# A fused attention and token-mixing kernel: one load moved to ScalarE's queue, no filler between transposes, gate logits on VectorE, a narrower last eviction, and a new order of work

## The chip, the cores and the metric

The kernel runs on one core of a Trainium2 chip. A core has five engines that each work through a queue of their own: TensorE (PE in the profile; its weight loads are PEld), VectorE (DVE), ScalarE (ACT), GpSimd (POOL) and SyncE (SP), which here only issues DMAs. They wait for each other through semaphores. Data live in SBUF; matmuls write PSUM[...]. The time is device microseconds of one execution; the profile comes from one execution of its own, which was timed too.

## What is computed

x has 2048 tokens (S) of 512 channels (D), in bf16. Two branches are blended by a gate for each token.

```python
# A: causal attention in a sliding window of 256 tokens, 32 heads of 16 channels
q, k, v = split(x @ wqkv)                       # wqkv 512 x 1536
scores = einsum(q, k) * 16 ** -0.5              # kept where 0 <= query - key < 256
a = (softmax(scores) @ v).reshape(S, D) @ wo    # wo 512 x 512

# B: an MLP that mixes tokens
h = layernorm(x)                                # over channels, no weights
u = gelu(einsum("bsd,sf->bdf", h, w1) + b1)     # w1 2048 x 1376
y = (einsum("bdf,fs->bds", u, w2) + b2).transpose(0, 2, 1)   # w2 1376 x 2048

g = sigmoid((x * gate_w).sum(-1, keepdims=True))
out = g * a + (1 - g) * y
```

## The kernel before

**A list of tasks and an order written out.** The program is a list of tasks, each made by `add(name, {engine: cost}, emit, deps, ...)`: a group of instructions of one engine, the tasks it needs, the buffers or PSUM banks it takes, and a guess of its cost. `arrange(tasks)` at L85 puts them in order. It doesn't choose the engine or the order on an engine: both stand in `PLAN`, a table with one list of names per engine, in which a digit behind a colon is the PSUM bank or buffer to take. The set `THEN` names the steps after which a matmul step of 512 columns is issued in four row tiles of 128 x 32 (`tiled`) instead of one of 128 x 128. Costs and constants (`SWITCH`, `LATENCY`, `FETCH` and others) only steer in which sequence instructions of different engines are emitted and what the search for `PLAN` saw.

**The start.** x is loaded in groups of 128-token tiles by `load_x` (L449, DMA at L454): the first 512 tokens as x0.0 (tokens 0 to 255) and x0.2 (256 to 511), 256 KB each, the others as 512 KB. The query and key columns of wqkv come as four loads of 256 KB (wqk0 to wqk3, L470), the value columns as one (wv, L475). Everything goes out on SP's queue. The transposed x that the projections need is made by TensorE for the first 512 tokens (`emit_xt`, L605: 128 x 128 transposes, L608) and by transposing DMAs for the rest (xt1 to xt3, L463). TensorE begins with five matmuls of 512 zero columns (`warming`, L589, matmul at L591), which read the block `zeros` of 512 columns (L363, cleared at L518). Four transpose tasks of four 128 x 128 blocks follow, two for each half of the 512 tokens; between the halves stands `warmb`, three more matmuls of 256 zero columns. Each transpose task is copied out of PSUM by `copy_out` (L598, on ScalarE L602 or on VectorE L603).

**The middle.** `chain` (L655) makes every accumulation over several matmuls: projections q, k, v, the MLP's u (11 blocks of 128 features) and y (16 tiles of 128 tokens), each cut into steps of two matmuls that `PLAN` interleaves; all are recorded at L670. Attention runs in 16 query tiles and a few more groups: scores (s, L942, L998, L1042), exponentials on ScalarE (e, L894), masks on GpSimd or VectorE (m, L536, L974), weighted values (pv, L1087), then normalization by VectorE (n1 to n4 and nz, L1178 to L1213, which transpose back). Query evictions are multiplied by a parity column (QZ, L754). Layernorm statistics are L770 to L780. Evictions of the other projections and u may be on either engine (L438, L440, L602, L603).

**The gate.** For the first `NGP` = 1 block of 512 tokens the logits are 16 one-column matmuls (`emit_gate`, L799 to L805, recorded at L802; eviction L812). For the other tokens each 128-token tile is one fused multiply and sum on VectorE, task gl, L822. Then come an exponential (gatee) and the weights of the blend, c1 and c2.

**The end.** A y chain has 11 matmuls over features and four over wo and the normalized attention. f (L441 on VectorE, L438 on ScalarE) evicts it with c1 and c2, and o (L1305) stores it. The last tile is done in two halves of 256 columns, `y15l` and `y15r`.

## Time and profile before

| | |
|---|---|
| median of three runs | 200.57 us (199.84 to 200.81) |
| the profiled execution, timed | 199.82 us |
| its span, first to last instruction | 198.1 us |
| first matmul starts | 1.38 us |
| x0.0 landed, first transpose | 3.74, 3.79 us |
| first projection starts | 6.57 us |
| last matmul ends, about | 195.0 us |
| granted TensorE clock, mean | 1.00 |

Each line of the waits' view names an engine, its operation and what ended its wait, then total us, times and longest. A timeline line has start, duration, engine, line of the code, operation, and the operands with their shapes; a square bracket gives idle time ahead of it and what ended it. A group's row has total busy us and mean ns of one instruction. Durations of neighbours may overlap[...]; the time between two starts is the cost of one.

### The profile page before, as it was taken

What the parts mean: (1) busy time and instruction counts of PE and PEld (TensorE: products, weight loads), DVE (VectorE), ACT (ScalarE), POOL (GpSimd) and SP (SyncE); (2) the same over time, 40 slices, a digit from 0 to 9 for tenths busy, and PEclk for the clock granted to TensorE, in tenths of its full rate; (3) what the DMA queues carried; (4) which work ended last, traced back from release to release, by engine and by line L of the source; (5) the groups of instructions that cost most, each with busy time, mean ns of one, the idle gap of its engine ahead of it and who ended that gap; (6) DMA issues with size and microseconds to landing.
All of it is one profiled execution on the core that took longest, in us unless ns stands there. A gap on an engine that the chain in (4) does not pass through costs nothing. (4 is left out here: it accounts for less than half of the span.)

```text
span 198.1 us, 9100 instructions
## 1 busy us (share of the span) xinstructions
PE 193.0 (97%) x4058; PEld 93.3 (47%) x4058; DVE 156.5 (79%) x318; ACT 169.0 (85%) x198; POOL 80.0 (40%) x118
## 2 busy tenths in 40 slices
PE   7999999999999999999999999999999999999993
PEld 3643444353635445446543554344445354554572
DVE  1799888879998988986589799636867868869683
ACT  2369999999988996998999899899899989898632
POOL 6394897525344440214223200045069335452310
PEclk9999999999999999999999999999999999999999
DMA  5999798970060000001399770000211220200002
GB/s 156 294 284 232 131 319 278 346 187 0 8 174 18 18 0 3 3 5 32 98 364 367 280 210 3 26 26 30 68 37 58 60 68 22 62 30 30 30 3 83
DMA packets 23189, 22.02 MB, mean 111 GB/s; under 512 B 7566, under 2 KB 21262, under 8 KB 23150
## 3 DMA queue, kind: packets, MB, share of 16 engines
q1 hardware_dynamic: 23150, 21.44, 36.9%
q8 instruction: 32, 0.52, 1.1%
q14 instruction: 7, 0.06, 0.1%
HBM read 15.61 MB, written 2.10 MB: 89 GB/s over the span
## 5 line engine op out<-in xcount | busy, mean ns | idle before, releaser
L894 ACT ACTIVATE et<-ps 128x1024 bf16<-128x1024 f32 (+1 forms) x94 | 89.3, 1015 | 6.1 <-PE ps L942 2.4
L536 POOL TENSOR_SCALAR_AFFINE_SELECT et<-et 128x512 bf16<-128x512 bf16 (+2 forms) x63 | 46.7, 751 | 56.0 <-ACT et L894 40.9
L894 ACT ACTIVATE XT<-ps 128x1024 bf16<-128x1024 f32 (+1 forms) x60 | 58.1, 1011 | 7.3 <-PE ps L942 4.3
L670 PEld LDWEIGHTS <-wb 128*32 128x32 bf16 (+4 forms) x645 | 32.0, 97 | 34.5 <-issue 6.5
L670 PE MATMUL pb<-ug,wb 128*32 128x512 bf16 (+4 forms) x385 | 45.5, 366 | 0.0
L670 PE MATMUL pb<-h,wb 128*128 128x512 bf16 (+2 forms) x260 | 44.5, 381 | 0.0
L536 POOL TENSOR_SCALAR_AFFINE_SELECT XT<-XT 128x512 bf16<-128x512 bf16 (+1 forms) x28 | 20.0, 720 | 46.3 <-ACT XT L894 27.4
L670 PE MATMUL pb<-XT,wqkv 128*128 128x512 bf16 (+2 forms) x190 | 32.4, 372 | 0.4 <-DMA wqkv<-in_A_wqkv_dram 0.3
L1178 DVE STREAM_TRANSPOSE et<-ps 128x1024 f32<-128x1024 f32 (+1 forms) x17 | 20.1, 1183 | 11.9 <-PE ps L1087 11.1
L1087 PEld LDWEIGHTS <-VA 128*32 128x32 bf16 (+1 forms) x1056 | 20.1, 97 | 6.6 <-issue 1.5
L942 PE MATMUL ps<-QZ,KT 32*128 32x256 bf16 (+1 forms) x496 | 23.1, 265 | 0.0
L754 DVE TENSOR_TENSOR QZ<-pb,par 128x1024 bf16<-128x1024 f32 x16 | 19.5, 1221 | 3.2 <-PE pb L670 3.2
L670 PEld LDWEIGHTS <-wqkv 128*128 128x128 bf16 (+1 forms) x190 | 12.7, 98 | 14.6 <-DMA wqkv<-in_A_wqkv_dram 0.5
L670 PE MATMUL pb<-wo,xo 128*32 128x512 bf16 (+2 forms) x152 | 18.1, 375 | 0.0
L1087 PE MATMUL ps<-et,VA 128*32 128x128 bf16 (+2 forms) x624 | 17.9, 218 | 0.0
L942 PEld LDWEIGHTS <-KT 32*128 32x128 bf16 x496 | 7.4, 92 | 20.6 <-ACT et L894 10.7
L670 PE MATMUL pb<-wqkv,XT 128*128 128x512 bf16 (+1 forms) x70 | 16.5, 381 | 0.0
L974 DVE TENSOR_TENSOR et<-et,mask 128x512 bf16<-128x512 bf16 x26 | 13.3, 510 | 2.5 <-ACT et L894 2.4
L441 DVE TENSOR_SCALAR ot<-pb,c,c 128x512 bf16<-128x512 f32 (+1 forms) x11 | 8.6, 785 | 7.4 <-PE pb L670 7.3
L1087 PE MATMUL ps<-XT,VA 128*32 128x128 bf16 (+2 forms) x432 | 13.9, 215 | 0.0
L1087 PEld LDWEIGHTS <-VZ 128*32 128x32 bf16 x832 | 13.2, 98 | 0.7
L770 DVE BATCH_NORM_STATS2 stats<-xo 128x6 f32<-128x512 bf16 x16 | 10.7, 682 | 3.1 <-DMA xo<-in_A_x_dram 3.1
(76 smaller groups left out, 199.4 us busy)
## 6 DMA issues: line engine op xcount, KB each, us to landing
wb<-in_B_w_dram SPq DMA_DIRECT2D x8, 512.0 KB, 8.2
wb<-in_B_w_dram SPq DMA_DIRECT2D x2, 2048.0 KB, 9.2
VZ<-VA SPq DMA_DIRECT2D x26, 70.0 KB, 3.0
xo<-in_A_x_dram SPq DMA_DIRECT2D x3, 512.0 KB, 5.5
out_dram<-ot SPq DMA_DIRECT2D x12, 128.0 KB, 2.4
wb<-in_B_w_dram SPq DMA_DIRECT2D x4, 352.0 KB, 5.8
wqkv<-in_A_wqkv_dram SPq DMA_DIRECT2D x4, 256.0 KB, 5.0
wb<-in_B_w_dram SPq DMA_DIRECT2D x1, 1024.0 KB, 5.3
```

Source lines behind the costliest of these rows:

```text
L441: return nc.vector.tensor_scalar(out=out_, in0=in_, scalar1=scale, scalar2=bias, op0=ALU.mult, op1=ALU.add)
L536: return nc.gpsimd.affine_select(out=out_, in_=in_, pattern=[[0, n] for n in pattern] + [[step, HB]], compare_op=op, fill=0.0, base=base_, ...
L670: made.append(nc.tensor.matmul(buf(b)[c:z_, c0:c0 + w_], lhsT=lhsT[:, c:z_], rhs=rhs, start=(j == 0), stop=(j == n - 1), skip_group_check= ...
L754: lambda k=k, b=b: nc.vector.tensor_tensor(out=QZ[:, k, :, (i % NQ) * SB:(i % NQ + 1) * SB], in0=buf(b)[:, None, :].to_broadcast([P, 2, SB ...
L770: f"bs{t_}", {"DVE": 0.67}, lambda b=b, t_=t_: nc.vector.bn_stats(buf(b)[:], xo[:, t_, :]),
L894: lambda e=e, b=b, shape=shape: nc.scalar.activation(out=shape(buf(e)), in_=shape(buf(b)), func=ACT.Exp, scale=SCALE),
L942: made.append(nc.tensor.matmul(to[:, :, done:done + m], lhsT=keys(j if x == "A" else j - 1, k)[rows], rhs=q[rows], start=True, stop=True, ...
L974: made.append(nc.vector.tensor_tensor(out=v, in0=v, in1=m.to_broadcast(list(v.shape)), op=ALU.mult))
L1087: return lambda: nc.tensor.matmul(to(), lhsT=v() if callable(v) else v, rhs=buf(e)[rows, col:col + n], start=first, stop=last, tile_positi ...
L1178: lambda: nc.vector.transpose(out=view(buf(tr).bitcast(FP32)), in_=view(buf(o))), [last], takes=[tr], uses=[o],
```

## The change

The DMA of x0.2 is issued by ScalarE instead of SP, as the first instruction in ScalarE's list. The filler `warmb` between the transposes is gone. `zeros` has 128 columns, and the five warm-up matmuls read them repeated. `NGP` is 0, so the logits of the first four tiles are made by four more gl tasks on VectorE and no matmuls. The last tile is done in three parts of 256, 128 and 128 columns (l, m, r). `arrange` gets other costs: a price `TURN` for each pair of matmul forms instead of one `SWITCH`, `cost_of`, and another model of instruction fetch. `PLAN` and `THEN` are new throughout.

What the new lists do: on SP, gate_w and wv now come right after x1.4 and ahead of the transposing loads (before: x1.4, xt1, wv, x2.8, ...). Three of the four copies of transposed x are on VectorE (before: one). Thirteen evictions move from VectorE to ScalarE and as many back; 28 masks move from GpSimd to VectorE and 29 the other way. Value projections come earlier among the first projections. There are 3997 matmuls instead of 4058, and 167 changes of matmul form from step to step instead of 169.

```diff
-SWITCH = 0.095
+TURN = {
+    "d": dict(d=0, s=0.100, p=0.100, c=0.098, h=0.100),
...
+def cost_of(t, e):
...
 PLAN = dict(
     PE="""
-        warm:3 xta0.0.0:7 xta0.0.1:6 warmb xta0.1.1:4 xta0.1.0:5 q1_0.0:2 k3_0.0:3 k1_0.0:6 q3_0.0:1 k0_0.0:7
...
-        y14.11 y14.13 y13.13 y15r.6 y15r.8 y15l.11 y15l.13 y15r.10 y15r.11 y15r.13
+        warm:3 xta0.0.0:5 xta0.0.1:4 xta0.1.0:7 xta0.1.1:3 q1_0.0:0 q0_0.0:1 k3_0.0:6 q3_0.0:2 k1_0.0:5
+        k1_0.1 q0_0.1 k0_0.0:7 k1_0.2 k2_0.0:3 k2_0.1 k0_0.1 q1_0.1 k0_0.2 q3_0.1 q3_0.2 q3_0.3 k3_0.1
...
+        y15r.4 y15r.6 y14.13 y15l.4 y15l.6 y15l.8 y15l.10 y15l.11 y15l.13 y15m.0:4 y15r.8 y15r.10 y15r.11
+        y15r.13 y15m.2 y15m.4 y15m.6 y15m.8 y15m.10 y15m.11 y15m.13
     """,
     ACT="""
-        xtc0.0.1 xtc0.1.0 xtc0.1.1 kc3_0 kc1_0 kc0_0 kc2_0 e0.v0.0:4 e0.v0.1:5 kc3_1 e0.C.1:8 e0.C.0:a e-1.C.1:7
...
+        x0.2 xtc0.0.0 kc3_0 kc0_0 kc1_0 kc2_0 vc1 e0.v0.1:9 e0.v0.0:8 vc0 kc2_1 e0.C.1:1 e0.C.0:2 vc5
...
     DVE="""
-        const zeros bs3:1 xtc0.0.0 bs2:0 ba3 parity bs1:1 ba2 ba1 bs0:0 ba0 qc1_0 bs4:1 qc0_0 ba4 qc3_0 qc2_0 qc3_1
...
+        zeros bs1:1 bs3:0 ba3 bs0:0 xtc0.1.0 ba0 xtc0.1.1 bs2:0 ba1 xtc0.0.1 ba2 const parity qc3_0 bs6:0
...
     SP="""
-        x0.0 x0.2 wqk0 wqk1 wqk2 wqk3 x1.4 xt1 wv x2.8 bias xt3 x3.12 xt2 vs0 w1_02 w1_03 vs1 w1_22 vs2 gw w1_12
...
+        x0.0 wqk0 wqk1 wqk2 wqk3 x1.4 gw wv xt1 xt3 x3.12 x2.8 bias vs0 xt2 vs1 w1_11 w1_12 w1_00 w1_10
...
-    NGP = 1
+    NGP = 0
...
-    zeros = ug[:, 0, :]
+    zeros = ug[:, 0, 0:P]
...
                 src = X[t0 * P:(t0 + n_) * P].rearrange("(t p) d -> p t d", t=n_)
+                if t0 == 2:
+                    nc.scalar.dma_start(xo[:, t0:t0 + n_, :], src)
+                    return
                 nc.sync.dma_start(xo[:, t0:t0 + n_, :], src)
...
-            nc.tensor.matmul(buf(wu)[:, 0:w], lhsT=zeros[:, 0:P], rhs=zeros[:, 0:w], start=True, stop=True)
+            nc.tensor.matmul(
+                buf(wu)[:, 0:w].rearrange("p (a b) -> p a b", b=P), lhsT=zeros,
+                rhs=zeros[:, None, :].to_broadcast([P, w // P, P]), start=True, stop=True,
+            )
...
-    between = None
     for n_ in range(2):
-        if n_:
-            between = add("warmb", {"PE": 0.64}, lambda: warming(3, 256), [t], uses=[wu], ins=6)
...
-        parts = [("", 0, D)] if t_ < NT - 1 else [("l", 0, D // 2), ("r", D // 2, D)]
+        parts = [("", 0, D)] if t_ < NT - 1 else [("l", 0, D // 2), ("m", D // 2, 3 * D // 4), ("r", 3 * D // 4, D)]
```

## The prediction

> **What bounds the kernel now.** I read the page's busy shares first, then the waits of TensorE, then the timeline of its first and last microseconds, then windows, and last the rows of the operations that the change touches.

> ```profile
> span 198.1 us, 9100 instructions
> PE 193.0 (97%) x4058; PEld 93.3 (47%) x4058; DVE 156.5 (79%) x318; ACT 169.0 (85%) x198; POOL 80.0 (40%) x118
> ...
> PE pb L591 <- DVE ug L518: 1.4, 1, 1.4
> ...
> PE pb L670 <- DMA wqkv<-in_A_wqkv_dram: 0.3, 1, 0.3
> ...
> PE pb L670 <- ACT XT L894: 0.2, 1, 0.2
> ```

> The span is that of one profiled execution, timed at 199.82 us: 1.72 us lie outside it. TensorE is busy 97%, and its matmuls' listed waits (us in all, times, longest) are the 1.4 us before the first one, 0.3 us for the first weights and 0.2 us for an exponential. So a saving must come from TensorE's own work, from its start, or from what follows its last matmul. ScalarE may come next:

> ```profile
> 20.00:30.00 10.00, 10.00 (x110) 4.24 (x109) 8.68 (x28) 9.79 (x15) 8.96 (x15) 1.00 0.87 221
> ```

> This is a row of the windows view: PE, weight loads, DVE, ACT and POOL busy in 10 us, then clock, DMA share and GB/s. TensorE is full, ScalarE has 0.21 us left, and the DMA engines are at 0.87.

> The start, from the timeline (start, duration, engine, line):

> ```profile
> 3.79 1.03 PE L608 MATMUL pb<-ident,xo 128*128 128x128 bf16 x8
> 4.62 0.85 PE L591 MATMUL pb<-ug 128*128 128x256 bf16 x3
> 5.26 1.06 PE L608 MATMUL pb<-ident,xo 128*128 128x128 bf16 x8
> 6.57 7.25 PE L670 MATMUL pb<-XT,wqkv 128*128 128x256 bf16 x40 [0.26 <-DMA wqkv<-in_A_wqkv_dram]
> ...
> 4.44 0.69 DVE L770 BATCH_NORM_STATS2 stats<-xo 128x6 f32<-128x512 bf16 x1 [3.12 <-DMA xo<-in_A_x_dram]
> ...
> 0.81 0.97 SPq L454 DMA_DIRECT2D xo<-in_A_x_dram  x2
> 1.82 1.88 SPq L470 DMA_DIRECT2D wqkv<-in_A_wqkv_dram  x4
> 4.23 5.73 SPq L463 DMA_TRANSPOSE XT<-in_A_x_dram  x1
> 10.01 0.57 SPq L475 DMA_DIRECT2D wqkv<-in_A_wqkv_dram  x1
> ```

> The reader is to see that the first projection waits for weights, not for transposes, so the filler (three matmuls at 4.62) stands in time that TensorE has to wait anyway. A transposing DMA also holds SP's queue for 5.73 us, and the load of wv stands behind it.

> The gate's logits on TensorE, and what VectorE pays for the same (row: busy, mean ns):

> ```profile
> 23.02 0.54 PE L802 MATMUL pb<-gwc,XT 128*128 128x1 bf16 x16
> 23.43 1.02 PE L670 MATMUL pb<-wqkv,XT 128*128 128x512 bf16 x4
> ...
> L822 DVE SCALAR_TENSOR_TENSOR junk<-xo,gwr 128x512 bf16<-128x512 bf16 x12 | 8.3, 695 | 0.1
> L822 DVE DVE_READ_ACCUMULATOR junk<-xo,gwr 128x1 f32 x12 | 1.0, 81 | 0.0
> ```

> The end: the last matmuls stop at 195.04, and one eviction and one DMA follow.

> ```profile
> 191.21 0.72 DVE L1178 STREAM_TRANSPOSE et<-ps 128x512 f32<-128x512 f32 x1 [0.53 <-PE ps L1087]
> ...
> 193.85 0.60 PE L670 MATMUL pb<-wo,xo 128*128 128x256 bf16 x4
> 195.04 0.55 DVE L441 TENSOR_SCALAR ot<-pb,c,c 128x256 bf16<-128x256 f32 x1 [0.61 <-PE pb L670]
> ```

> [...] a 512-column matmul takes 427 ns in the warm-up and 216 ns later, and the 256-column projections drop from about 213 to 109 ns at 6.92 us. [...] Issues on SP stand 0.51 us apart, and the engines are 0.99 busy from 5 to 10 us; no run here shows a load from ScalarE. [...]

> **The change, part by part.** All sums stand against the profiled execution, 199.82 us; the median of the three shown runs, 200.57, is 0.75 above it.

> *Gate on VectorE.* TensorE loses 23.43 − 23.02 = 0.40 us, on the path: **−0.40**. VectorE gains 4 × (0.695 + 0.081) = 3.1 us. It stood idle in 21% of the span, but the four come before about 20 us, among the q evictions (1.22 us each) that free PSUM banks for the projections. With cover gone I would pay one such wait of at most 0.78. I take 0 for it, range 0 to +0.8.

> *Filler.* −0.64 us of TensorE's work (3 × 0.213), worth 0 while the projection waits for weights. [...]

> *x of tokens 256 to 511 from ScalarE.* SP no longer issues it, so the first weights are issued one slot (0.51 us) earlier, at 1.32. But the bytes are unchanged: x0.0, x0.2 and the first weights are 256 KB each on the same engines, and the weights (issued 1.82) landed at 6.53, the rest about 0.65 apart. Bounds 0 and −0.5; I take **−0.10**. x0.0 landed at 3.74 and x0.2 at 4.41; sharing from the start, x0.0 may come up to 0.67 later, inside the same cover of 0.26 + 0.64. On ScalarE the issue (about 0.5 us) comes ahead of everything, when it has nothing to do.

> *Copies of the transposes.* In before, one of the four runs on VectorE and three on ScalarE; now three run on VectorE, behind batch statistics. By its rows (0.69 each, the next starting 0.61 to 0.65 later): statistics of tiles 1, 3 and 0 from 3.8, copies of 0.41 from about 5.9 and 6.3, another statistics, and the last copy at about 7.4 to 7.9. Projections over that half of the channels are in PE's order from about 7.3. A new wait of 0 to 0.5; I take **+0.30**.

> *Form changes and order.* TensorE's steps are switches between tile forms: two matmuls of 512 columns take 0.432 before a step of the same form and 0.527 before another. The order goes from 169 to 167 switches and exchanges some tiled steps; with the median of each kind of step in the trace, the steps other than gate and filler sum to **−0.18**. Two gaps of before (0.33 in all at 113 us, 0.13 at 143) came from banks held by exponentials at just those places. The new order puts other steps there and may open gaps of its own; from −0.46 to +0.8, I take **−0.20**.

> *Moves between ScalarE and VectorE.* 13 evictions go each way, of near equal length (copies of 0.4 to 0.8); masks go 28 to VectorE and 29 to GpSimd. Net nothing where TensorE leads.

> *SP's order.* wv goes ahead of the first transposing DMA and its 5.73 us. Values are computed from 12.6 us instead of 16.6, by summing step durations from 6.5, and wv should land near 12. Behind it the xt1 load slips by the two loads put ahead of it: 0.64 MB at 291 GB/s is 2.2 us, from 12.06 to about 14.3; it is first used at 15.6. xt3 follows with an issue of 3.2 to 4.3 us, so about 17 to 18; first used at 17.6. Bounds 0 and +0.8, I take 0. wo, w1 and the exchanges of V are reordered by several us, against uses from 45 us on; nothing.

> *Tail.* The last eviction has 128 columns: 0.81 for 512 and 0.55 for 256 extrapolate to 0.41: −0.14; the last matmul is 0.05 shorter: **−0.19**. The one chain of 256 is now two of 128; a weight load with a one-column matmul took 25 ns in the gate, so loads don't bind (0.04, inside the −0.18). But fewer filler steps stand between the last pv step (190.64) and the tail that needs its normalized tile: 2.4 us by step durations, where the trace had 2.93, and VectorE's chain from 191.21 ended at 193.37, 2.46 with the pv step's end: **+0.15**.

> Zeros on 128 columns halve a memset of 0.27; TensorE starts about 0.15 earlier, and that is covered by x0.0. Sum: −0.40 − 0.10 + 0.30 − 0.18 − 0.20 − 0.19 + 0.15 = **−0.62 us**: 199.2 beside the profiled execution, and with the 0.75 a median of about 199.9.

> **The rivals.** About 0.5%, 1.0 us, is what a measurement of this kernel can tell from no change.

> *A, faster by more.* The copies cost nothing (−0.30), the weights land 0.5 earlier (−0.4 more), the old gaps go without new ones (−0.26): −1.58, so 199.0. For it: TensorE follows its own steps within 2.4 us over the whole trace. Against it: the DMA engines' 0.99 at the start.

> *C, ScalarE takes over.* With 9.79 of 10 us busy, exponentials set when banks come free, and TensorE's 0.58 turns into waits on ET and XT in 20 to 50 us: 200.5. Against it: the matmuls list 0.2 us of waits for exponentials in the whole span.

> *B, slower: [...]* The release at 6.92 followed a window of 3.41 us [...]:

> ```profile
> 3.51:6.92 3.41, 3.06 (x22) 2.36 (x22) 2.48 (x8) 1.16 (x3) 0.41 (x2) 1.00 0.91 299
> 0.10:3.51 3.41, 2.13 (x5) 0.58 (x5) 0.45 (x4) 1.28 (x1) 2.67 (x14) 1.00 0.42 126
> ```

> TensorE was 90% busy in it[...]. Without 0.64 us of filler the same window has 2.42 of 3.41, 71%; earlier projections may refill a few points. [...] matmuls stay at half speed until 10.3 us: 3.4 us at half rate lose 1.7. The copies' +0.30 is then hidden. −0.62 − 0.30 + 1.7 = +0.8: 201.4. [...]

> **How the numbers follow.** Forecast 0.40, own range 199.4 to 200.4; A 0.28; C 0.10; B 0.22, which stands also for a late xt3. Faster by over 0.5% (under 199.57): A and a quarter of the forecast's share, 0.38. Same: the rest of the forecast and C, 0.40. Slower: B, 0.22. The range 198.6 to 201.5 leaves out the outer parts of A and B.

> **What would show it.** The L802 row gone and L822 at 16; the first projection at 6.4 to 6.5; 256-column projections at 0.11 us from about 6.9 (B: from 10.3); a wait of PE for the XT copy of VectorE near 7.4 to 9; the wait of the last "wo" matmuls of the first part for VectorE, 0.1 to 0.2; a 128-column last eviction of 0.41. The forecast is wrong if TensorE's busy time outside the start doesn't fall by about 0.6, or if waits for xt3 or for banks of exponentials over 0.5 us stand in the middle.

## The result, and the profile after

The change makes the kernel slower: 202.47 us median (201.90 to 202.75) against 200.51 (199.84 to 200.81), ratio 1.0112, 95% interval 1.0086 to 1.0138. The time lies above the predicted range. Medians are of all timed executions of a kernel, while ratios leave out those over 1.5% above the kernel's fastest, so the two need not agree. The profiled execution took 202.45 us, its span is 200.7. First the page of the changed kernel, its busy shares and its DMA queues:

```profile
span 200.7 us, 8968 instructions
...
PE 192.7 (96%) x3997; PEld 92.4 (46%) x3997; DVE 155.6 (78%) x326; ACT 168.8 (84%) x198; POOL 73.6 (37%) x117
...
q8 instruction: 31, 0.51, 1.0%
q10 hardware_dynamic: 272, 0.26, 0.4%
```

```profile
PEld L979 <- issue: 3.4, 6, 1.4
...
PEld L1124 <- issue: 3.3, 5, 1.9
...
PE ps L1124 <- issue: 1.7, 1, 1.7
PE ps L979 <- issue: 1.2, 1, 1.2
...
PE pb L707 <- DMA wqkv<-in_A_wqkv_dram: 0.6, 1, 0.6
```

"issue" is time in which the engine waited for nothing that the profile shows. In the kernel before, the longest such wait on these two lines (there L942 and L1087) was 0.4 us. The timeline shows the places (start, duration, then engine, line and operands):

```profile
5.68 6.69 PE L707 MATMUL pb<-XT,wqkv 128*128 128x256 bf16 x36
12.95 1.02 PE L707 MATMUL pb<-wqkv,XT 128*128 128x512 bf16 x4 [0.58 <-DMA wqkv<-in_A_wqkv_dram]
...
40.82 0.11 PEld L979 LDWEIGHTS <-KT 32*128 32x128 bf16 x5
42.33 0.10 PEld L979 LDWEIGHTS <-KT 32*128 32x128 bf16 x3 [1.40 <-issue]
...
116.43 0.21 PEld L1124 LDWEIGHTS <-VA 128*32 128x32 bf16 x11
118.50 0.09 PEld L1124 LDWEIGHTS <-VA 128*32 128x32 bf16 x1 [1.86 <-issue]
```

A step of scores is cut in the middle at 40.8 us, after five of eight weight loads, and a step of weighted values at 116.6 us. The profile shows no semaphore that ended either wait. The account, from start to start of matmuls and against the usual length of each kind of step in the trace of before:

| | before | changed | difference |
|---|---|---|---|
| first projection starts | 6.57 | 5.68 | −0.89 |
| wait for wv at 12.0 us | 0 | 0.74 | +0.74 |
| gap at 40.8 us | 0 | 1.39 | +1.39 |
| gap at 116.6 us | 0 | 1.87 | +1.87 |
| all else from first projection to last matmul | | | −0.19 |
| from last matmul's end to the end | 3.10 | 2.78 | −0.32 |
| span | 198.1 | 200.7 | +2.6 |

The −0.19 is less than the 0.58 that the step lengths gave; the rest sits in waits of under 0.2 us each, which I can't assign.

Two facts led to a theory. Counting TensorE's instructions in program order (weight loads, matmuls and the few waits), the gap at 40.8 stands behind number 960 = 3 × 256 + 192, the one at 116.6 behind number 4289 = 16 × 256 + 193. And the instruction queue was late just there. The DMA view of the changed kernel, window 112.5 to 116 us, has no transfer on q8 at all (first two lines); the window 116 to 117 us has one (last two):

```profile
DMA packets 259, 1.05 MB, mean 300 GB/s; under 512 B 3, under 2 KB 3, under 8 KB 259
...
q1 hardware_dynamic: 259, 1.05, 87.3%
...
q1 hardware_dynamic: 93, 0.32, 102.5%
q8 instruction: 1, 0.02, 5.8%
```

By the transfers' own records it began at 116.04 and took 0.94 us, and TensorE went on at 118.50. The one before the gap at 40.8 began at 39.91 and ended at 40.99; TensorE went on at 42.33. The trace doesn't show when a block is asked for. The changed planner's constant AHEAD puts it 77 instructions ahead of a block's end, and this place is taken as an estimate of the request from here on; the trace fits it roughly: 22 of the 31 transfers begin 0.6 to 1.8 us after it, and seven begin 3.1 to 3.9 us after it, with loads filling the DMA engines (their share 0.85 to 1.06). Two more (at 119.6 and 127.3 us) begin 3.1 and 3.3 us after it though few or no loads ran, which stays open. The planner's other constants fit the trace too: BLOCK 256 the count of transfers, INSIDE 194 the gaps behind 192 and 193. **Theory:** dense stretches of small matmuls use up a block before a transfer that stands behind bulk loads has brought the next. **Rival:** an unseen wait for data, a bank or another engine, and the wait for wv or VectorE's new work as the true loss.

### The profile page after: what moved, and what is told of

Same layout as the page of the kernel before. It is cut to its first block, busy times and chain, and to the rows that moved or that the text cites. A ratio compares the mean times of both kernels' runs of the same rounds, so it can differ in the third digit from the quotient of the medians.

```text
span 200.7 us, 8968 instructions
## 1 busy us (share of the span) xinstructions
PE 192.7 (96%) x3997; PEld 92.4 (46%) x3997; DVE 155.6 (78%) x326; ACT 168.8 (84%) x198; POOL 73.6 (37%) x117
## 4 chain that ended last, share of the span: by engine, by line
PE 91%; DMA 6%; issue 2%; DVE 0%
PE pb L707 67%; PE ps L1124 11%; PE ps L979 10%; DMA wqkv<-in_A_wqkv_dram 4%; PE ps L1079 3%; DMA xo<-in_A_x_dram 2%; PE ps L1035 0%; DVE ot L475 0%; PE pb L593 0%
## 5 line engine op out<-in xcount | busy, mean ns | idle before, releaser
L931 ACT ACTIVATE et<-ps 128x1024 bf16<-128x1024 f32 (+1 forms) x105 | 100.0, 1022 | 8.4 <-PE ps L979 4.7
L573 POOL TENSOR_SCALAR_AFFINE_SELECT et<-et 128x512 bf16<-128x512 bf16 (+2 forms) x63 | 41.9, 680 | 79.0 <-ACT et L931 41.2
L931 ACT ACTIVATE XT<-ps 128x1024 bf16<-128x1024 f32 (+1 forms) x49 | 46.5, 1003 | 5.1 <-PE ps L979 2.8
L707 PE MATMUL pb<-ug,wb 128*32 128x512 bf16 (+6 forms) x327 | 46.0, 367 | 0.0
L707 PE MATMUL pb<-h,wb 128*32 128x512 bf16 (+2 forms) x308 | 44.8, 381 | 0.0
L573 POOL TENSOR_SCALAR_AFFINE_SELECT XT<-XT 128x512 bf16<-128x512 bf16 (+2 forms) x27 | 18.5, 692 | 36.6 <-ACT XT L931 22.9
L707 PE MATMUL pb<-wo,xo 128*32 128x512 bf16 (+3 forms) x144 | 17.9, 368 | 0.0
L1215 DVE STREAM_TRANSPOSE et<-ps 128x1024 f32<-128x1024 f32 x11 | 13.7, 1245 | 4.7 <-PE ps L1124 4.4
L1124 PE MATMUL ps<-et,VZ 128*32 128x64 bf16 x608 | 13.8, 193 | 0.0
L944 DVE TENSOR_TENSOR et<-et,mask 128x1024 bf16<-128x1024 bf16 (+1 forms) x19 | 12.5, 673 | 0.8 <-ACT et L931 0.7
(77 smaller groups left out, 199.0 us busy)
```

Source lines behind the costliest of these rows:

```text
L573: return nc.gpsimd.affine_select(out=out_, in_=in_, pattern=[[0, n] for n in pattern] + [[step, HB]], compare_op=op, fill=0.0, base=base_, ...
L707: made.append(nc.tensor.matmul(buf(b)[c:z_, c0:c0 + w_], lhsT=lhsT[:, c:z_], rhs=rhs, start=(j == 0), stop=(j == n - 1), skip_group_check= ...
L931: lambda e=e, b=b, shape=shape: nc.scalar.activation(out=shape(buf(e)), in_=shape(buf(b)), func=ACT.Exp, scale=SCALE),
L944: return nc.vector.tensor_tensor(out=v, in0=v, in1=m[:, None, :].to_broadcast([P, n, w]), op=ALU.mult)
L1124: return lambda: nc.tensor.matmul(to(), lhsT=v() if callable(v) else v, rhs=buf(e)[rows, col:col + n], start=first, stop=last, tile_positi ...
L1215: lambda: nc.vector.transpose(out=view(buf(tr).bitcast(FP32)), in_=view(buf(o))), [last], takes=[tr], uses=[o],
```

## Experiments

Medians are of the timed runs; ratios are to the kernel before on the same chip.

**Holding back a bulk load (e1, e5).**

```diff
-emit, m1[4 * g:4 * g + 4]
+emit, m1[4 * g:4 * g + 4] + ([x for x in tasks if x.name == "pv8.2"] if g == 2 else [])
```

> The changed kernel, with one dependency more: the last load of w2 (blocks 8 to 10, about 0.5 MB) waits until the step pv8.2 is done, so that the DMA engines are idle when TensorE's instructions for the block around 116 us are fetched. Theory, late instructions: the gap of 1.9 us inside step pv7.3 at 116.6 us goes (under 0.3 us is left), the transfer on the instruction queue starts about 1 us after TensorE passes the place that asks for it and not 3.5 us, the gap at 40.8 us stays; time about 200.7 us, ratio to the kernel before about 1.002. Rival, a wait for data, a bank or VectorE that the profile does not show: the gap stays at 1.9 us and the time at 202.5, or grows where y steps wait for the later w2.

201.65 us, ratio 1.0073 (1.0048 to 1.0098). A task's dependencies only steer the planner; the semaphores come from the tiles. The load went out at 112.96, and the gaps stayed at 1.2 and 1.8 us. The run is a near repeat of the changed kernel, on another chip: there wv landed at 12.25 and TensorE didn't wait for it. But the clock also came later, at 7.2 us instead of 6.1, so TensorE reached the first value projection at 12.70, against 12.95 behind the wait. Only 0.25 us of the 0.74 came back. In e5 the wait is a real one:

```diff
+            if t.name == "pv8.2":
+                held = final
+            if t.name == "w2_2":
+                tc.add_manual_dep(first, held.name, ...)
```

> The changed kernel; the last load of w2 (about 0.5 MB) now waits by a semaphore for the last matmul of pv8.2, at about 116.5 us (in run e1 the edit only moved the order in which instructions were written out, and the load went out at 112.96 as before). Theory, late instructions: the instruction transfer that started at 116.04, 3.5 us after TensorE passed the place that asks for it, starts within 1.3 us of it, and the gap of 1.7 to 1.9 us goes; the gap at 40.8 stays; time 1.5 to 1.9 below that of e1 (201.65), about 200.0 us, ratio 0.999. Rival, a wait for data or a bank: the gap stays and the time with it.

201.30 us, ratio 1.0060 (1.0038 to 1.0082). The window 112.5 to 117.5 us of e5 (PE, weight loads, DVE, ACT, POOL busy; clock, DMA share, GB/s):

```profile
112.50:117.50 5.00, 5.00 (x226) 3.13 (x221) 3.65 (x6) 4.32 (x5) 3.16 (x5) 1.00 0.01 3
```

With DMA at 0.01, TensorE is busy for all 5 us, and the instruction transfer begins at 113.94, 1.0 us after it is asked for instead of 3.6. The gap is gone with no other input of the step changed: the rival falls there. The time fell less than expected. In the profiled run the clock came at 8.7 us instead of 6.1, and a new wait stands at 124.8 us, 0.79 over the step's usual length: scores of tile 9 for exponentials that come after the gelu. The gap had stood in front of it.

**Less traffic around 41 us (e2), v1 later (e3), together (e4).**

```diff
-        vz6:1 vs2 w1_02 w1_03 w1_01 wo w1_13 ...
-        vz7:0 w2_0 ...
+        vz6:1 vs2 w1_02 w1_03 w1_01 w1_13 ...
+        vz7:0 wo w2_0 ...
```

> The changed kernel with the 0.5 MB load of wo moved on SP from 35 us to just ahead of the first load of w2 (about 95 us), so that the bulk loads end some 1.5 us sooner around 41 us. Theory, late instructions: the transfer on the instruction queue that started at 39.91 starts about 1.4 us sooner, and the gap of 1.4 us inside s2.v0 at 40.8 us shrinks to under 0.3; the gap at 116.6 stays; time about 201.2 us, ratio about 1.004. Rival, s2.v0 waits for an exponential or a bank: the gap stays at 1.4 and the time at 202.5.

201.57 us, ratio 1.0080 (1.0048 to 1.0111); profiled span 199.4. The transfer ended at 39.71 and the excess of s2.v0 fell from 1.39 to 0.50. A smaller effect than expected: it still began 2.9 us after it was asked for. Four loads of w1 had been issued from 33.47 to 35.83 us, so wo's was not the only one ahead of it.

```diff
-k1_0.4 v1.0:2 v1.2 q2_0.1 q2_0.2 s0.v0:04 q2_0.3 q2_0.4 v0.0:7
+k1_0.4 q2_0.1 q2_0.2 s0.v0:04 q2_0.3 q2_0.4 v1.0:2 v1.2 v0.0:7
```

> The changed kernel with the first value projection (v1.0, v1.2) moved on TensorE behind q2_0.4, five steps later, so that it comes when wv has landed. Theory, wv's landing at 12.9 is what holds TensorE at 12.0: the gap of 0.74 us goes and the time falls by 0.5 to 0.7, to about 201.9 us, ratio 1.008; both gaps in the middle stay. Rival, the next projections wait for the evictions of the first ones anyway: a wait of the same size appears in the steps ahead of v1.0 and the time stays at 202.5.

204.55 us, ratio 1.0191 (1.0135 to 1.0247): a miss, and the rival's case. In place of 0.74 us for wv there are waits of 0.59 us (scores, for VectorE) and 0.74 us (keys of the next block, for ScalarE); the trace of e4 has the same two. It seems that v1 was work that TensorE could do while the queries were evicted. The profiled execution of e3, the longest of its four, also fell to half clock for 3.41 us behind the gap at 118 us (see the last section).

> The changed kernel with the three edits of the runs beside it together (last w2 load held back, wo loaded late, v1 later). If the three gaps are the whole loss, they give back 1.9 + 1.4 + 0.6 = 3.9 us: about 198.6 us, ratio 0.990, and the rest of the change (start 0.9 earlier, 1.4 us less of TensorE's work, shorter tail) shows as a gain against the kernel before. If the gaps only hide other waits, the time stays above 200.5.

203.85 us, ratio 1.0154 (1.0098 to 1.0211). It carries e3's waits and, with the edit of e1, no held load; it decides nothing more.

**The same kernel before, with 64 more instructions (e7).** This is the test of the theory where nothing of the change is present.

```diff
-    add("warm", {"PE": 2.2}, lambda: warming(5, 512), ...)
+    add("warm", {"PE": 2.2}, lambda: warming(37, 64), ...)
```

> The kernel before, in which the warm-up's five matmuls of 512 zero columns are 37 matmuls of 64, in the same time and ahead of a wait for x: 64 more TensorE instructions at the start and nothing else. Theory, TensorE's instructions come in blocks of 256 and a dense stretch just ahead of a block's position 192 stalls if the block's transfer is late: the same dense stretches now fall elsewhere in the blocks, and gaps of 0.5 to 2 us appear inside steps, always at position 192 or 193 of a block, first of all around 61, 75, 112 to 117, 150 and 168 us; 3 to 8 us slower, 203 to 208 us. Rival, the gaps in the changed kernel come from its own order and data: nothing happens, 200.1 us within 0.4.

210.06 us, ratio 1.0399 (1.0348 to 1.0450). The profiled execution took 207.45, its span is 205.7. Two lines of weight loads in its timeline, of two different steps:

```profile
97.47 0.33 PEld L670 LDWEIGHTS <-wb 128*32 128x32 bf16 x11 [1.45 <-issue]
...
122.65 0.10 PEld L1087 LDWEIGHTS <-VZ 128*32 128x32 bf16 x2 [1.50 <-issue]
```

Six gaps of 0.7 to 1.6 us from matmul to matmul stand in it behind instructions 3521, 3776, 4545, 5825, 6849 and 8129: number 192 or 193 of a block each time. Their sum is 7.4 us, against 7.6 us that the span grew by. TensorE goes on 1.3 to 1.6 us after the end of the block's transfer at all six, as in the changed kernel. Of the five places named ahead three came true, 4 to 8 us later in this longer run (121, 156 and 176 us), and two didn't (61 and 75); 96, 103 and 198 us were not named. The time was over the 203 to 208 that I had named: 32 more matmuls in time that was free cost 4%.

These gaps also correct the theory. Bulk loads were in the way at only two of the six (103 and 121 us, with the DMA engines at 0.71 and 0.94 between request and transfer). At the other four the engines' share was 0.4 or less and the transfer began 0.8 to 1.1 us after the estimated request. There TensorE ran through the 270 or so instructions from request to stop in 1.7 to 2.6 us, which was faster than even a prompt block came. So a dense stretch alone can be enough.

**Parts of the change, in the kernel before (e8, e10 to e14).**

```diff
-        x0.0 x0.2 wqk0 ...
+        x0.0 wqk0 ...
+                if t0 == 2:
+                    nc.scalar.dma_start(xo[:, t0:t0 + n_, :], src)
+                    return
```

> The kernel before with one part of the change alone: x of tokens 256 to 511 loaded from ScalarE's queue. From the two profiles: the first weights land at about 4.95 and not at 6.53, so the first projection starts when filler and transposes are done, at about 6.15 instead of 6.57. Theory, the whole order moves 0.4 us earlier: about 199.7, ratio 0.998. Rival, wv (landed 14.65) or a late block of instructions gives it back: 200.1 within 0.3, with a new gap in the profile.

199.88 us, ratio 0.9979 (0.9963 to 0.9996): as expected. The first projection starts at 6.00, 0.57 earlier.

e10 takes out `warmb` alone, which also takes six instructions (three weight loads and three matmuls) out of the count.

> The kernel before without the filler between the transposes. Theory, the filler stands in a wait for the first weights (6.53): the first projection still starts at 6.5 to 6.6 and the time stays at 200.1 within 0.4. Rival from the prediction, [...] 256-column projections at 0.21 us until about 10 us, and 1 to 1.7 us slower, 201.5.

202.47 us, ratio 1.0074 (1.0048 to 1.0100), from 199.47 to 204.72, and by the medians of all executions 1.0124; the profiled run was the fastest and shows no late block. Neither expectation explains such a spread. e13 is the same kernel once more, and e14 has the warm-up as 8 matmuls of 320 columns to keep every later instruction in its place:

> The kernel of e10 once more, for its trace: 19 of its 20 runs took 201 to 205 us, and the one that was traced 199.5. Theory, the clock is released late in most runs: 256-column projections at 0.21 us apart until about 9 to 10 us, 1.3 us and more behind e10's trace. Rival, late instructions: six instructions fewer ahead of every later one have moved a dense stretch onto position 192 of a block, and a gap of over 1 us stands there, with the clock released by 7 us.

> The kernel before without the filler, with the warm-up in 8 matmuls of 320 columns and not 5 of 512, so that all later TensorE instructions keep their places in their blocks. If the late clock makes e10 slow, this is as slow: 202 us and as scattered. If the places of the instructions did, this is 200.0 within 0.4.

e13 took 203.04 us in its one execution. Its clock was released early, at 4.9 us; its waits are of the other kind, and wqkv came late:

```profile
PEld L1085 <- issue: 4.0, 7, 1.8
...
PE ps L1085 <- issue: 2.3, 2, 1.6
PEld L668 <- DMA wqkv<-in_A_wqkv_dram: 1.8, 2, 1.1
```

Its two longest gaps inside steps, 1.8 us at 94.7 and 0.9 us at 90.1, stand behind number 193 of a block (3265) and number 193 or 194 (3009 or 3010), counted by weight loads since 32 matmul records are missing in this trace. With places kept, e14 has 200.76 us, ratio 1.0025 (1.0002 to 1.0047): most of e10's loss was six instructions of shift. But e14's profiled run, 201.81 us, shows the late clock too: 256-column projections stand 0.21 us apart until 10.1 us. So the late clock of the prediction's rival B exists; how often it comes, one trace a kernel can't tell. For the changed kernel and its variants (all without filler) the release read off the spacing of matmuls was at 6.1 (changed), 7.2 (e1), 6.2 (e2), 8.7 (e5), 6.8 (e6), 4.7 (e9), 7.1 (e15) and 8.3 us (e16).

e11 moves the gate's first logits to VectorE behind `ba10`, loads gate_w behind wv and adds 16 matmuls to the warm-up.

> The kernel before with the gate's first logits on VectorE (four more fused multiply-sums, gate_w loaded behind wv) instead of 16 matmuls; 16 matmuls are added in the warm-up at no time, so that the later TensorE instructions keep their places in their blocks. Theory: TensorE loses 0.40 us on its path, 199.7 us, ratio 0.998. Rival, four times 0.78 us of VectorE at 21 us hold evictions that free banks: a gap on TensorE near 22 to 30 us and no gain, or up to 0.8 us slower.

203.84 us, ratio 1.0181 (1.0124 to 1.0238): the rival, and worse than it said. The weighted values at 29 us waited 2.04 us, and TensorE then ran for 3.41 us at half clock (last line, a row of the windows view):

```profile
27.73 0.20 ACT L837 ACTIVATE ez<-ez 128x4 f32<-128x4 f32 x1 [2.14 <-DVE ez L831]
...
28.99 0.19 PE L1087 MATMUL ps<-et,VA 64*32 64x64 bf16 x1 [2.04 <-ACT XT L894]
...
30.53:33.95 3.42, 3.42 (x16) 1.02 (x15) 2.29 (x13) 3.13 (x4) 1.91 (x4) 0.50 1.00 331
```

The four sums fill VectorE from 24.2 to 27.5 us. ScalarE has the gate's exponential next in its list (first line) and stands idle for 2.14 us until they are done, and the exponentials of scores, which the weighted values need, come behind it. The gate_w load also stands ahead of x's. In the changed kernel, whose order was made with the sums, no such wait is seen. The part is good or bad by where it is put.

> The kernel before, in its own order, with three parts of the change: x of tokens 256 to 511 from ScalarE's queue, no filler, gate logits on VectorE (16 matmuls of the warm-up keep the places of later instructions). If the parts add: 0.9 us from the start and 0.4 from the gate, 198.9 us, ratio 0.9935. If the start's gain is given back to wv, or VectorE is late: 199.6 to 200.1.

205.29 us, ratio 1.0245 (1.0193 to 1.0296). It has the gap of e11 (2.7 us between two matmuls here), 3.41 us at half clock, and a gap of late instructions, 1.8 us behind number 3265 = 12 × 256 + 193. The warm-up makes up for the gate's instructions but not for the filler's six, so the places are shifted as in e10. Of the three parts only the load had gained alone; the other two had each lost.

**The changed kernel mended (e6, e9, e15, e16).** e6 joins e5 and e2 and issues wv ahead of gate_w.

> The changed kernel with the last w2 load held back as in e5, wo loaded late as in e2, and wv issued ahead of gate_w on SP (instead of moving v1). Theory: both gaps of late instructions go (1.8 and 1.2 us below e1's 201.65) and TensorE waits for wv at most 0.3 us at 12 us; 198.6 us, ratio 0.992, so the rest of the change is a gain of about 1.5 us against the kernel before. Rival, waits behind the gaps take their place: above 200.

200.94 us, ratio 1.0047 (1.0024 to 1.0070). The wait for wv and the gap at 116 went; the one at 40.5 came back (1.38), as the transfer again began 3.5 us after it was asked for. e9 keeps these edits, sends three loads of w1 out earlier, and holds w2 for a shorter time (its lines beside those of the changed kernel and of e6):

```diff
-        vz6:1 vs2 w1_02 w1_03 w1_01 wo w1_13 ...
+        w1_02 w1_03 w1_01 vz6:1 vs2 w1_13 ...
-x.name == "pv8.2"
+x.name == "k0_3.2"
```

> The changed kernel with the bulk loads moved away from the two late blocks: the loads of w1 that went out at 33 us go ahead of the exchanges of V they stood behind (the engines were nearly idle from 31 to 34 us), so that they are done when TensorE asks for instructions at 36 us; the last w2 load waits for k0_3.2 (about 115 us), after the fetch of that block and 1.5 us sooner than in e5, so that y0.8 need not wait for it; wo late and wv ahead of gate_w as in e6. Theory: no gap over 0.3 us inside a step, both instruction transfers start within 1.5 us of being asked for; 2 us below e6 (200.94), about 198.9 us, ratio 0.993. Rival, late loads or V exchanges take the place of the gaps: above 200.

199.48 us, ratio 0.9975 (0.9962 to 0.9988): faster than before, and 1.5 us faster than e6. The waits of e9's TensorE by the same view:

```profile
PEld L979 <- issue: 1.7, 4, 0.4
PEld L1124 <- issue: 1.5, 4, 0.4
...
PE ps L979 <- ACT et L931: 0.7, 1, 0.7
...
PE pb L707 <- DVE XT L643: 0.6, 1, 0.6
```

No gap of late instructions is left, at the same TensorE instructions in the same order; the two transfers began 2.1 and 0.9 us after they were asked for. Two other waits are: for exponentials after the gelu, and for a copy of transposed x.

> Run e9 with the three copies of transposed x on VectorE put ahead of two of the batch statistics. In e9's profile TensorE waited 0.6 us for the first of them at 5.8. They are ready 0.6 to 0.8 us sooner: the wait falls under 0.2, time about 199.1 us, ratio 0.9955. If wqk1 or the later statistics take over, it stays at 199.5.

199.44 us, ratio 0.9962 (0.9946 to 0.9979): not to be told from e9. In its profiled run no copy was late, but the clock came at 7.1 us instead of 4.7, so the projections were slower too and the edit's own share can't be told.

> Run e15 with four score steps of tile 9 (s9.v3, s9.v2, s9.C, s9.v0) each moved on TensorE one to two y steps later. In e9 and e15, with the late instructions gone, TensorE stood 0.72 to 0.79 us at s9.v3 for exponentials that come after the gelu on ScalarE. Theory: y steps fill that time, the gap falls under 0.3 us, about 198.8 us, ratio 0.993. Rival, ScalarE sets the pace there and the wait moves to s9.v2 or later: 199.4.

200.52 us, ratio 1.0006 (0.9986 to 1.0026): no gain. The wait at s9.v3 is gone from the profile, but ScalarE's instructions behind the gelu run at the same distance from those ahead of it as in e15 (from its 169th to its 181st instruction 9.44 us, 9.35 there), so the wait was spread and not saved, which speaks for ScalarE's work setting the pace there. Its profiled run also had the clock only at 8.3 us, 0.6 us later at the first scalar copies. Its ratio against e15's isn't explained beyond that.

## Why the prediction was wrong

- **The bound.** TensorE's own time was read rightly as the bound. What fails is "So a saving must come from TensorE's own work, from its start, or from what follows its last matmul": a loss could come from the supply of instructions, which the page of before showed as queue q8 with 32 transfers. I took the diff's model of instruction fetch for a matter of the planner and did not price it.
- **The step that failed: "Form changes and order".** I let the new order's gaps lie "from −0.46 to +0.8" and took −0.20, as waits for banks. The trace has 1.39 + 1.87 = 3.26 us, and e5, e7 and e9 show that they are late blocks of instructions: they go when bulk loads are moved, and come at number 192 or 193 of other blocks when instructions are added. Without these 3.26 us, and with nothing in their place, the changed kernel would stand near 199.2, below the kernel before; e9 has 199.48.
- **x of tokens 256 to 511.** −0.10 in bounds of 0 to −0.5 was too small: −0.89 between the two profiles, filler's removal included, −0.57 in e8 alone. The prediction allowed for the issue time only, 0.51 us. Measured, it was more: the first weights landed at 4.95 instead of 6.53, 1.58 earlier. Before, they had landed 2.12 us behind the load ahead of them (x0.2, 4.41), where the next ones were 0.65 apart. Now the second part of the weights comes late, 1.53 us behind the first (6.48). Why one of the first loads is held up is not known.
- **SP's order.** wv "should land near 12", with first use at 12.6: it landed at 12.91 in the profiled run, and TensorE came at 12.0 since the start had moved. Of 0.89 us won at the start, 0.74 was given back there. In e1 there was no wait, but by its later clock TensorE came only at 12.70. xt1 and xt3 held nothing up, as said.
- **Gate.** The 0.40 us left TensorE, and in the changed order VectorE had the room. e11 shows that this cover is the order's doing. Elsewhere the part cost 2.5 and 3.2 us in the two executions at full clock, beyond my bound of 0.8, and 4.5 and 4.6 in the two that fell to a mean clock of 0.992. The wait I named was for evictions; the one that came was ScalarE's, for the logits.
- **Copies on VectorE.** +0.30 was a fair size: 0.15 in the changed kernel with the clock released at 6.1 us, 0.6 in e9 with the release at 4.7.
- **Filler.** That it is "worth 0 while the projection waits for weights" no longer helped, as the weights landed at 4.95. With the filler (e8) the first projection starts at 6.00, straight behind the transposes; without it, in the changed kernel, at 5.68. So 0.32 of the 0.89 us seems to be the filler's. It also holds the place of six instructions, which I had not thought of.
- **Tail.** −0.19 + 0.15; the end came 0.32 sooner after the last matmul, and VectorE held the last weight loads of the 256-column part for 0.15. The last eviction took 0.41, as extrapolated.
- **Rival B**, a later release of TensorE's clock, had the sign of the result by another mechanism: in the profiled execution, which took about the median time, the clock came at 6.1 us, earlier than the 6.9 before. What I let the release depend on is shown by no run here; e14 shows only that it can come as late as 10.1 us, near the 10.3 I had named. **Rival C** was a real wait behind the gap at 116.6, 0.7 us, not the time of the whole.

## What to carry to other kernels

Where TensorE runs thousands of small instructions back to back (7994 here), count them: if the profile shows waits for "issue" in the middle of a step that are far longer than the rest (gaps of 0.7 to 1.9 us here; at most 0.4 us for such a wait in the kernel before), compare their places in the program modulo 256, the block that fits the 31 transfers here, and look at what bulk loads run when the instruction queue is late. Where loads stand in the way, moving them by a few microseconds mended it here (e5, e9). Where none do, as at four of e7's gaps, that can't help, and no run here tried to mend such a gap. When comparing variants, keep the number of instructions ahead of each point the same, or the shift is measured instead of the edit.

## What the runs showed that I had not expected

- 64 more instructions in idle time made a kernel of 200 us 4% slower (e7); six fewer cost 0.7% (e10), and most of that went with the places restored (e14).
- After a late transfer's packets end, TensorE goes on 1.3 to 1.5 us later (40.99 to 42.33, 116.97 to 118.50), and 1.3 to 1.6 at the six gaps of e7.
- A long gap can cost twice. In the traces of e3, e11 and e12 TensorE stood between two matmuls for 2.4, 2.4 and 2.7 us, and from 121.30, 30.53 and 28.10 us, within 1.6 us of the gap's end, the granted clock was 0.50 for 3.41 us. In e11 the executions with a mean clock of 0.992 took 204.50 and 204.64 us, those with 1.000 took 203.17 and 202.45: about 1.8 us apart, where 3.41 us at half rate lose 1.7. The two longest executions of e7 have 0.992 too. Behind the gap of 1.9 us in the changed kernel, and one of 2.2 in e4, no such stretch is seen; what sets it off isn't shown.
- The clock column of the windows view reads 1.00 even ahead of the first release (0 to 6.1 us in the changed kernel), though 256-column matmuls stand 0.21 us apart there and 0.11 us afterwards. The release has to be read off their spacing.
- The release of TensorE's clock wandered from 4.7 to 10.1 us in the traces without filler; what sets it isn't shown. Among the changed kernel and its variants, whose starts are nearly the same, the releases lie between 4.7 and 8.7 us.
